# Scores of an attention kernel in half-array matmuls, and weighted values in one bank

## The chip, the cores and the metric

The kernel runs on one core of one Trainium2 chip. The metric is the device time of one execution in microseconds (us), as the median of several runs. One execution is also recorded by the hardware profiler; the profile below belongs to that one.

## The reference, cut to what matters

```python
# q, k, v: (8 batches, 12 heads, 448 positions, 64 wide), all float32
q_n, k_n = rmsnorm(q, g_q), rmsnorm(k, g_k)          # over the 64
scores = 1/8 * q_n @ k_n.T                            # 448 x 448 per head
attn = softmax(scores)
x = (attn @ v), heads side by side                    # (8*448, 768)
h = x @ w_in                                          # 768 -> 2048
g = h * clip(h + 3, 0, 6) / 6
out = g @ w_out                                       # 2048 -> 768, float32
```

There are 96 heads and, behind them, a feed-forward network on 3584 rows.

## The kernel before, in words

**Pairs.** Heads are worked on in 48 pairs: head A and head B of a pair, 6 pairs to a batch (`HP`). The 448 positions of a head are three tiles of 128 and a rest of 64 (`NT`, `REST`). k, q and v come in for two pairs at a time (`load_k`, `load_q`, `load_v`, L254 to L277, queue of SP). POOL squares, DVE sums, ACT makes the inverse root, and the normalised k and q are written as bf16.

**Transposes.** Scores need k and q with the 64 features on the partitions. For pairs 0 to 13 (`TD = 14`) PE transposes (L349) into one bank `t_ps`, and DVE or ACT copies out. From pair 14 on, that is heads 28 and later, one transposing DMA per pair does it (`transposes_dma`, L378): it takes 11 blocks of 128 x 128, seven of k and four of q, from a staging tile and puts them into one of three `kq` tiles. ACT then multiplies the transposed q by the gains (`scale_q`, L375).

**Scores.** The seven k blocks are padded: blocks 0 to 2 hold head A on partitions 0 to 63 and zeros below, blocks 4 to 6 hold head B on partitions 64 to 127 and zeros above, block 3 holds the rests of both. q has both heads, A above B. So each of seven matmuls per pair (`score`, L393, 128 keys x 448 queries, contraction over 128 partitions) gives the scores of one head, or of the two rests. POOL writes the padded blocks in two multiplications (`normalize_k`, L359), q in one (`normalize_q`, L367); the zeros are set once (`clear_kq`, L525). Scores go to two PSUM banks `sc` in turn, and ACT takes the exponential of each out of its bank (`expo`, L399, into a ring of 14 tiles `eT`).

**Weighted values.** `weigh` (L413, L419) multiplies the exponentials by v with a column of ones, for all four query tiles of a pair: 28 matmuls, in two halves of 14, into two banks `av`. `divide` (L428, L429) takes the reciprocal of the sums and multiplies, on DVE. The result `xn` is transposed into `xT` by PE for pairs 0 to 13 (`x_out`, L446, with a DVE copy, L457), by DMA from then on (`x_out_dma`, L450).

**Feed-forward.** When six pairs of a batch are done, its 16 blocks of h can run (`h_mm`, L461, six matmuls of 448 columns each), each with a clip on ACT (`relu`, L467) and a product on DVE (`gate`, L472), and then y (`y_mm`, L480, 16 matmuls of 384 columns each), copied out (L280) and stored (L491). These use three banks `m`, and at the end also the two `sc` banks. PSUM's eight banks are so: `sc` 2, `m` 3, `av` 2, `t_ps` 1.

**What sets the order.** Each engine works through a fixed list of instructions. The lists come from a planner (`Plan`, L46 to L154) that runs when the kernel is built: every step has an engine (or a choice of them), an assumed duration, the steps that it needs, and a key for its priority. `Plan.run` plays the steps through in assumed time and hands each engine what is ready. On PE, attention's steps come first and feed-forward matmuls fill the gaps, kept to a ratio (`share`); after 110 us of assumed time a PE step is taken only 500 ns after the step of another engine that it needs (`STEADY`, `SLACK`).

Of the kernel before, what the change touches and what calls it, by code (L numbers as in the profile page):

```python
# [8 lines left out]
FP32 = mybir.dt.float32  # L9
# [148 lines left out]
def kernel(  # L158
# [32 lines left out]
    TD = 14  # L191
    W4 = 4 * P
# [18 lines left out]
    kpad = [x[:, 0:7 * P] for x in kq_r]  # L211
    sq_r = ring(2, [P, GP, 8, D], FP32, "sq")
# [4 lines left out]
    qT_r = [x[:, 7 * P:7 * P + S] for x in kq_r]  # L217
    eT_r = ring(NE, [P, W4], BF16, "eT")
# [6 lines left out]
    KQ = 11 * P // 2  # L225
# [5 lines left out]
    sc_r = ring(2, [P, 512], FP32, "sc", psum)  # L231
    m_r = ring(3, [P, 512], FP32, "m", psum)
    av_ps = psum.tile([P, 4, 256], FP32, name="av")
    t_ps = psum.tile([P, 2, 4 * P], BF16, name="t_ps")
# [13 lines left out]
    def part_of(p, n):  # L248
        return (p // GP) % NS, slice(p % GP, p % GP + n)
# [12 lines left out]

    def load_k(eng, p, n):
        g, pr = part_of(p, n)
        src, st = heads(k, p, n), k_st[g][:, pr]
        eng.dma_start(
            out=st.rearrange("p r h t d -> p (r h) (t d)")[:, :, 0:NT * D], in_=blocks(src))
        for rows, x, t, rest in zip((lo, hi), (0, 0), (NT, 4), halves_of(src)):
            eng.dma_start(out=st[rows, :, x, t, :], in_=rest)
# [34 lines left out]
    def raw(a, p, n):  # L304

        g, pr = part_of(p, n)
        return (k_st, q_st)[a][g][:, pr].rearrange("p r h t d -> p r (h t) d")[:, :, 0:8, :]
# [47 lines left out]
    def normalize_k(eng, p):  # L355
        blocks = kq_st[p % NQ][:, 0:7 * P]
        for h in range(2):
            c0 = h * (NT * P)
            eng.tensor_tensor(  # L359
                out=blocks[:, c0:c0 + W4].rearrange("p (t c) -> p t c", t=4)[:, :, h * D:(h + 1) * D],  # L360
                in0=raw(0, p, 1)[:, 0, 4 * h:4 * h + 4, :],
                in1=rstd_r[(p // GP) % 2][:, 0, p % GP, 4 * h:4 * h + 4].unsqueeze(2)
                .to_broadcast([P, 4, D]), op=A_MULT,
            )

    def normalize_q(eng, p):
        eng.tensor_tensor(  # L367
            out=kq_st[p % NQ][:, 7 * P:11 * P].rearrange("p (t h d) -> p h t d", t=4, h=2),
            in0=raw(1, p, 1).rearrange("p r (h t) d -> p (r h) t d", h=2),
            in1=rstd_r[(p // GP) % 2][:, 1, p % GP, :].rearrange("p (h t) -> p h t", h=2)  # L370
            .unsqueeze(3).to_broadcast([P, 2, 4, D]), op=A_MULT,
        )

    def scale_q(p):
        nc.scalar.activation(out=qT_r[p % NK], in_=qT_r[p % NK], func=COPY, scale=gprime[:])  # L375

    def transposes_dma(p):
        nc.sync.dma_start_transpose(  # L378
            out=kq_r[p % NK][:].rearrange("p (t c) -> p t c", c=P), in_=kq_st[p % NQ])

    def put_q(eng, p):
        if eng is nc.scalar:
            eng.activation(out=qT_r[p % NK], in_=t_ps[:, 1, 0:S], func=COPY, scale=gprime[:])
        else:
            eng.tensor_scalar_mul(qT_r[p % NK], t_ps[:, 1, 0:S], gprime[:])
# [6 lines left out]
    def score(p, i, n):  # L392
        nc.tensor.matmul(  # L393
            out=sc_r[n % 2][:, 0:S], lhsT=kpad[p % NK][:, i * P:(i + 1) * P],
            rhs=qT_r[p % NK], start=True, stop=True,
        )
# [7 lines left out]

    def weigh(p, half):
        va = vaug[p % NV]
        e = {i: eT_r[(7 * p + n) % NE] for n, i in enumerate(ORDER)}
        for i in (2 * half, 2 * half + 1):


            c0 = i * P if (p // HP) % 2 == 0 else (i * P - P if i else S - P)
            cols = slice(c0, c0 + P)
            nc.tensor.matmul(  # L413
                out=av_ps[:, i, 0:2 * W], lhsT=e[3][:, cols], rhs=va[:, 3].rearrange("p h d -> p (h d)"),
                start=True, stop=False, skip_group_check=True,
            )
            for t in range(NT):
                for h in range(2):
                    nc.tensor.matmul(  # L419
                        out=av_ps[:, i, h * W:(h + 1) * W], lhsT=e[4 * h + t][:, cols],  # L420
                        rhs=va[:, t, h], start=False, stop=(t == NT - 1 and h == 1),
                        skip_group_check=True,
                    )

    def divide(p):
        av4 = av_ps[:, :, 0:2 * W].rearrange("p n (h d) -> p n h d", h=2)
        rden = rden_r[p % 2]
        nc.vector.reciprocal(out=rden[:].unsqueeze(3), in_=av4[:, :, :, D:W])  # L428
        nc.vector.tensor_tensor(  # L429
            out=xn_r[p % NQ][:].rearrange("p n (h d) -> p n h d", h=2), in0=av4[:, :, :, 0:D],  # L430
            in1=rden[:].unsqueeze(3).to_broadcast([P, 4, 2, D]), op=A_MULT,
        )

    x_ps = t_ps[:].rearrange("p a c -> p (a c)")
# [90 lines left out]
    def clear_kq(eng, i):  # L525
        blocks = kq_st[i][:, 0:7 * P].rearrange("p (t c) -> p t c", c=P)
        eng.memset(blocks[:, 0:NT, D:P], 0.0)
        eng.memset(blocks[:, NT + 1:7, 0:D], 0.0)
# [11 lines left out]
    def at(xs, i):  # L540
        return xs[i] if 0 <= i < len(xs) else None

    sums, rst, nrm, vc, tr, pq, pk, scs, exs, wgh, div, xo, px = (
        [] for _ in range(13))

    def x_stage(p):
        b = p // HP
        if p >= TD:
            xo.append(plan.dma_transpose((p + 2, 0), 2 * P * W4, lambda: x_out_dma(p),
                               [div[p]] + h_ops.get(b - NX, [])[-1:]))  # L550
            px.append(xo[p])
            return
        xo.append(add((p + 2, 0), [("PE", 220, lambda: x_out(p))],
                      [div[p], at(px, p - 1)] + ([pq[p + 2], pk[2 * p + 4], pk[2 * p + 5]] if p >= HP else []),
# [92 lines left out]
    ckq = [by((2 * TD, 0), 600, 350, lambda e, i=i: clear_kq(e, i), w_ops[-NW:]) for i in range(NQ)]  # L647
# [4 lines left out]
    for p in range(NPAIR):  # L652
        g = p // GP
        if p % GP == 0:

            old = [nrm[i] for i in range(2 * (p - NS * GP), 2 * (p - NS * GP) + 2 * GP)] if g >= NS else [clr[g]]
            oldv = vc[p - NS * GP:p - NS * GP + GP] if g >= NS else [clv[g]]
# [19 lines left out]
            for j, (p0, n) in enumerate(single):  # L677
                j = min(j, len(todo) - 1)
                for a in range(2):
# [4 lines left out]
                             [(lk, lq)[a][j]] + ([squares[m - 2]] if m >= 2 else []))  # L684
# [22 lines left out]
        else:  # L707
            nrm.append(add((p - 2, 4), [("POOL", 1250, lambda p=p: normalize_k(G, p))],
                           [rstd_op[0, p], at(tr, p - NQ), ckq[p % NQ]]))
            nrm.append(add((p - 2, 4), [("POOL", 1100, lambda p=p: normalize_q(G, p))],  # L710
                           [rstd_op[1, p], at(tr, p - NQ), *w_ops[-NW:]]))
# [5 lines left out]
                      [lv[p], at(wgh, 2 * (p - NV) + 1), at(clo, p)]))  # L717

        if p >= TD:
            old = at(scs, 7 * (p - NK) + 6)  # L720
            tr.append(plan.dma_transpose((p - 1, 3), 22 * P * P, lambda p=p: transposes_dma(p),
                                         [nrm[2 * p], nrm[2 * p + 1], old]))
            pq.append(add((p - 1, 0), [("ACT", 640, lambda p=p: scale_q(p))], [tr[p], mg]))
            pk += [tr[p], tr[p]]
        else:
            tr.append(add((p - 1, 3), [("PE", 440, lambda p=p: transposes(p))],
                          [nrm[2 * p], nrm[2 * p + 1], at(px, p - 3) if p - 3 >= HP else None, at(pq, p - 1), at(pk, 2 * p - 1),
                           at(pk, 2 * p - 2)], 165))
            pq.append(add((p - 1, 0), [("DVE", 450, lambda p=p: put_q(V, p)), ("ACT", 640, lambda p=p: put_q(A_, p))],
                          [tr[p], mg, at(scs, 7 * (p - NK) + 6)]))  # L730
            for part in range(2):
                pk.append(add((p - 1, 1 + part), [("DVE", 415, lambda p=p, part=part: put_k(p, part))],
                              [tr[p], at(scs, 7 * (p - NK) + 6), at(clk, p)]))
        for n in range(7):
            i, m = ORDER[n], 7 * p + n
            scs.append(add((p, 2), [("PE", 189, lambda p=p, i=i, m=m: score(p, i, m))],
                           [pq[p], pk[2 * p], pk[2 * p + 1] if i >= 3 else None, at(exs, m - 2)], 165))
            exs.append(add((p, 1), [("ACT", 550, lambda m=m: expo(m))],
                           [scs[m], at(wgh, 2 * ((m - NE) // 7) + 1) if m >= NE else None]))
        for half in range(2):  # L740
            wgh.append(add((p + 1, 1), [("PE", 510, lambda p=p, half=half: weigh(p, half))],
                           exs[7 * p:7 * p + 7] + [vc[p], at(div, p - 1), pad], 165))
        div.append(add((p + 1, 0), [("DVE", 880, lambda p=p: divide(p))],
                       [wgh[2 * p], wgh[2 * p + 1], at(xo, p - NQ)]))
        if p >= 2:
            x_stage(p - 2)
            if p - 2 == HP - 1:
                plan.banks.append([m_r[2], px[HP - 1]])
            if p - 2 in (HP * b + HP - 1 for b in range(B - 1)):
                feed_forward((p - 2) // HP)  # L750
    x_stage(NPAIR - 2)
    x_stage(NPAIR - 1)
    plan.banks += [[m, exs[-1]] for m in sc_r]
# [35 lines left out]
```

## Time and profile before

| | us |
|---|---|
| runs shown: lowest, median, highest | 449.77, 450.78, 450.88 |
| the profiled execution's own time | 451.33 |
| its span in the profile | 449.5 |
| PE busy | 424.5 |
| ACT busy | 274.8 |
| DVE busy | 240.1 |
| POOL busy | 229.7 |
| matmuls of scores (L393): first and last start | 12.4, 364.2 |

The granted clock of TensorE was 0.995 on average. The span is what lies between the first and the last recorded instruction; the execution's own time is 1.8 us longer. Where the prediction shows lines of the profile: PE is TensorE with its matmuls, PEld its weight loads, DVE the vector engine, ACT the scalar engine, POOL GpSimd, SP the engine that issues most DMAs. A line with `xN` holds N instructions. A busy PE means that some matmul was under way; as matmuls overlap, the durations of single ones add up to more than the busy time. In the table of windows, each engine's busy time in a stretch stands with its number of instructions, then the granted clock, the share of time in which the 16 DMA engines moved data, and GB/s. In the list of waits, the columns are the waiting engine and its line, the releasing one, the total, how often, and the longest.

### The profile page before, as it was taken

What the parts mean: (1) busy time and instruction counts of PE and PEld (TensorE: products, weight loads), DVE (VectorE), ACT (ScalarE), POOL (GpSimd) and SP (SyncE); (2) the same over time, 40 slices, a digit from 0 to 9 for tenths busy, and PEclk for the clock granted to TensorE, in tenths of its full rate; (3) what the DMA queues carried; (4) which work ended last, traced back from release to release, by engine and by line L of the source; (5) the groups of instructions that cost most, each with busy time, mean ns of one, the idle gap of its engine ahead of it and who ended that gap; (6) DMA issues with size and microseconds to landing.
All of it is one profiled execution on the core that took longest, in us unless ns stands there. A gap on an engine that the chain in (4) does not pass through costs nothing.

```text
span 449.5 us, 9164 instructions
## 1 busy us (share of the span) xinstructions
PE 424.5 (94%) x3512; PEld 255.4 (57%) x3512; DVE 240.1 (53%) x428; ACT 274.8 (61%) x581; POOL 229.7 (51%) x251
## 2 busy tenths in 40 slices
PE   0888799899999989999999999999999999999996
PEld 0455366565566555666566565656565655555563
DVE  6899888845474346646444555453433253343321
ACT  2678678853487678878776777777767551132100
POOL 5899999958577766855667467552310000000000
PEclk9999899999999999999999999999999999999999
DMA  6899999981999999999899777955545210110021
GB/s 160 208 295 247 306 294 283 309 296 47 216 229 191 227 231 199 169 232 188 160 184 219 177 176 171 223 140 76 93 106 72 73 26 36 61 45 36 24 83 70
DMA packets 140908, 73.94 MB, mean 164 GB/s; under 512 B 90176, under 2 KB 137280, under 8 KB 140864
## 3 DMA queue, kind: packets, MB, share of 16 engines
q1 hardware_dynamic: 139232, 72.44, 69.3%
q10 hardware_dynamic: 1632, 0.92, 0.8%
q8 instruction: 27, 0.44, 0.4%
q14 instruction: 17, 0.14, 0.1%
HBM read 45.61 MB, written 11.01 MB: 126 GB/s over the span
## 4 chain that ended last, share of the span: by engine, by line
PE 84%; DMA 6%; POOL 2%; DVE 2%; ACT 2%; SPq 1%; issue 1%; POOLq 0%
PE m L461 29%; PE m L480 26%; PE sc L393 11%; PE av L419 7%; PE sc L480 5%; DMA k_st<-in_k_dram 4%; DMA kq<-w_st 3%; PE sc L461 3%; PE av L413 2%; ACT eT L399 2%; POOL qk L333 1%; POOL sq L315 1%; DVE vaug L280 1%; PE t_ps L349 1%; SPq L277 0%
## 5 line engine op out<-in xcount | busy, mean ns | idle before, releaser
L399 ACT ACTIVATE eT<-sc 128x448 bf16<-128x448 f32 x336 | 175.7, 542 | 48.6 <-PE sc L393 44.6
L461 PE MATMUL m<-xT,w_in_sb 128*128 128x448 bf16 x708 | 165.7, 355 | 0.2
L480 PE MATMUL m<-w_out_sb,gT 128*128 128x384 bf16 x768 | 150.0, 326 | 0.0
L393 PE MATMUL sc<-kq 128*128 128x448 bf16 x336 | 115.9, 359 | 8.2 <-ACT eT L399 6.4
L480 PEld LDWEIGHTS <-gT 128*128 128x128 bf16 x896 | 87.2, 98 | 62.3 <-issue 0.5
L461 PEld LDWEIGHTS <-w_in_sb 128*128 128x128 bf16 x768 | 74.1, 98 | 68.8 <-issue 6.0
L472 DVE SCALAR_TENSOR_TENSOR gT<-t_sb,m 128x448 bf16<-128x448 f32 x118 | 73.0, 620 | 72.9 <-ACT t_sb L467 72.4
L467 ACT ACTIVATE t_sb<-m 128x448 f32<-128x448 f32 x118 | 63.7, 541 | 47.3 <-PE m L461 44.3
L318 DVE TENSOR_REDUCE ssq<-sq 128x16 f32<-128x1024 f32 (+1 forms) x56 | 58.3, 1058 | 8.4 <-POOL sq L315 7.1
L359 POOL TENSOR_TENSOR w_st<-k_st,rstd 128x256 bf16<-128x256 f32 x68 | 40.2, 612 | 41.3 <-DMA kq<-w_st 40.6
L280 DVE COPY y_sb<-m 128x384 f32<-128x384 f32 x39 | 21.7, 557 | 61.4 <-PE m L480 61.2
L419 PE MATMUL av<-vaug,eT 128*128 128x65 bf16 x1152 | 54.5, 194 | 0.0
L419 PEld LDWEIGHTS <-eT 128*128 128x128 bf16 x1152 | 50.8, 99 | 4.4 <-issue 0.4
L315 POOL TENSOR_TENSOR sq<-k_st 128x1024 f32<-128x1024 f32 (+1 forms) x24 | 42.4, 1765 | 12.7 <-DMA k_st<-in_k_dram 5.9
L315 POOL TENSOR_TENSOR sq<-q_st 128x1024 f32<-128x1024 f32 (+1 forms) x26 | 44.5, 1710 | 7.1 <-DMA q_st<-in_q_dram 3.5
L393 PEld LDWEIGHTS <-kq 128*128 128x128 bf16 x336 | 31.3, 99 | 27.0 <-issue 4.9
L413 PE MATMUL av<-vaug,eT 128*128 128x130 bf16 x192 | 42.7, 222 | 0.0
L280 POOL CAST vaug<-v_st 128x512 bf16<-128x512 f32 x29 | 17.9, 618 | 45.2 <-PE av L419 44.6
L367 POOL TENSOR_TENSOR w_st<-q_st,rstd 128x512 bf16<-128x512 f32 x34 | 35.4, 1042 | 0.0
L429 DVE TENSOR_TENSOR xn<-av,rden 128x512 bf16<-128x512 f32 x48 | 33.2, 691 | 1.7
L428 DVE RECIPROCAL rden<-av 128x8 f32<-128x8 f32 x48 | 9.8, 205 | 34.1 <-PE av L419 33.7
L375 ACT ACTIVATE kq<-kq,gprime 128x448 bf16<-128x448 bf16 x34 | 22.6, 663 | 5.1 <-DMA kq<-w_st 5.1
(55 smaller groups left out, 222.5 us busy)
## 6 DMA issues: line engine op xcount, KB each, us to landing
out_dram<-y_sb SPq DMA_DIRECT2D x24, 384.0 KB, 2.9
k_st<-in_k_dram SPq DMA_DIRECT2D x23, 384.0 KB, 4.6
v_st<-in_v_dram SPq DMA_DIRECT2D x23, 384.0 KB, 4.6
q_st<-in_q_dram SPq DMA_DIRECT2D x22, 384.0 KB, 4.7
w_st<-in_moe_w_in_dram SPq DMA_DIRECT2D x8, 768.0 KB, 7.6
w_st<-in_moe_w_out_dram SPq DMA_DIRECT2D x8, 768.0 KB, 7.1
out_dram<-y_sb SPq DMA_DIRECT2D x8, 192.0 KB, 2.7
k_st<-in_k_dram SPq DMA_DIRECT2D x46, 32.0 KB, 3.9
```

What stands on the lines that cost most here:

```text
L280: (eng.copy if eng is nc.scalar else eng.tensor_copy)(out=out, in_=in_)
L315: eng.tensor_tensor(out=sq, in0=x, in1=x, op=A_MULT)
L318: nc.vector.tensor_reduce(out=ssq_r[(p // GP) % 2][:, a, p % GP:p % GP + n, :].rearrange("p r s -> p (r s)"), in_=sq_r[m][:, 0:n].rearrang ...
L359: eng.tensor_tensor(out=blocks[:, c0:c0 + W4].rearrange("p (t c) -> p t c", t=4)[:, :, h * D:(h + 1) * D], in0=raw(0, p, 1)[:, 0, 4 * h:4 ...
L393: nc.tensor.matmul(out=sc_r[n % 2][:, 0:S], lhsT=kpad[p % NK][:, i * P:(i + 1) * P], rhs=qT_r[p % NK], start=True, stop=True,)
L399: nc.scalar.activation(out=eT_r[n % NE][:, 0:S], in_=sc_r[n % 2][:, 0:S], func=EXP, bias=0.0, scale=1.0,)
L413: nc.tensor.matmul(out=av_ps[:, i, 0:2 * W], lhsT=e[3][:, cols], rhs=va[:, 3].rearrange("p h d -> p (h d)"), start=True, stop=False, skip_ ...
L419: nc.tensor.matmul(out=av_ps[:, i, h * W:(h + 1) * W], lhsT=e[4 * h + t][:, cols], rhs=va[:, t, h], start=False, stop=(t == NT - 1 and h = ...
L461: nc.tensor.matmul(out=m[:, 0:S], lhsT=w_in_sb[:, kt, f * P:(f + 1) * P], rhs=xT[:, kt, b % NX, x_slot(b)], start=(kt == 0), stop=(kt == N ...
L467: nc.scalar.activation(out=t[:], in_=m[:, 0:S], func=RELU, bias=0.5, scale=1.0 / 6.0,)
L472: nc.vector.scalar_tensor_tensor(out=gT[:, f, (b % 2) * S:(b % 2 + 1) * S], in0=t[:], scalar=1.0, in1=m[:, 0:S], op0=A_MIN, op1=A_MULT,)
L480: nc.tensor.matmul(out=m[:, 0:n], lhsT=gT[:, f, c0:c0 + P], rhs=w_out_sb[:, f, c:c + n], start=(f == 0), stop=(f == NFT - 1),)
```

## The change

From pair 14 on, the padded k blocks go. The staging tile has four blocks of k and four of q, each with head A on the first 64 features and head B on the other 64; the transposing DMA moves 8 blocks instead of 11. Two pairs are taken together as a group. A **burst** is four matmuls over 64 rows each: for each of two key tiles, head A on rows 0 to 63 and head B on rows 64 to 127, with q of the same rows, each into a bank of its own out of four. A group has three bursts; the rests of both pairs are two matmuls over 128 rows, with zeros where head A meets head B (`clear_late` sets them in the raw k tiles). ACT takes the exponential of two banks in one instruction. The four banks are the two of `sc`, that of `t_ps`, and one of `av`; so weighted values have one bank left from pair 13 (`AD`) on, and a half must be divided before the next half is written: `divide` runs per half. The outputs of pairs 12 and 13 (`XD`) are transposed by DMA too. At the end the four score banks, not two, serve feed-forward. In the planner a burst is given 620 ns, the two rests 378, a double exponential 960, a division of a half 580.

The core of the diff:

```diff
+    XD = 12
+    AD = 13
...
-    sc_r = ring(2, [P, 512], FP32, "sc", psum)
+    ps = psum.tile([P, 5, 512], FP32, name="ps")
     m_r = ring(3, [P, 512], FP32, "m", psum)
-    av_ps = psum.tile([P, 4, 256], FP32, name="av")
-    t_ps = psum.tile([P, 2, 4 * P], BF16, name="t_ps")
+    sc_r = [ps[:, i] for i in range(4)]
+    t_ps = ps[:, 2].bitcast(BF16).rearrange("p (a c) -> p a c", a=2)
...
+    def normalize_st(eng, p, a):
         eng.tensor_tensor(
-            out=kq_st[p % NQ][:, 7 * P:11 * P].rearrange("p (t h d) -> p h t d", t=4, h=2),
-            in0=raw(1, p, 1).rearrange("p r (h t) d -> p (r h) t d", h=2),
+            out=kq_st[p % NQ][:, a * W4:a * W4 + W4].rearrange("p (t h d) -> p h t d", t=4, h=2),
+            in0=raw(a, p, 1).rearrange("p r (h t) d -> p (r h) t d", h=2),
...
     def transposes_dma(p):
         nc.sync.dma_start_transpose(
-            out=kq_r[p % NK][:].rearrange("p (t c) -> p t c", c=P), in_=kq_st[p % NQ])
+            out=kq_r[p % NK][:, 0:8 * P].rearrange("p (t c) -> p t c", c=P), in_=kq_st[p % NQ])
...
+    def burst(jobs):
+
+        for i, (p, t) in enumerate(jobs):
+            for h in range(2):
+                rows = slice(h * D, h * D + D)
+                nc.tensor.matmul(
+                    out=sc_r[2 * i + h][:, 0:S], lhsT=kT_r[p % NK][rows, t * P:(t + 1) * P],
+                    rhs=qT_r[1][p % NK][rows], start=True, stop=True,
+                )
+
+    def rests(p):
+        for i in range(2):
+            nc.tensor.matmul(
+                out=sc_r[i][:, 0:S], lhsT=kT_r[(p + i) % NK][:, NT * P:W4], rhs=qT_r[1][(p + i) % NK],
+                start=True, stop=True,
+            )
+
+    def expo2(d, i):
+        nc.scalar.activation(
+            out=e2_r[d % (NE // 2)][:, :, 0:S], in_=ps[:, 2 * i:2 * i + 2, 0:S], func=EXP, bias=0.0,
+            scale=1.0,
         )
...
     def weigh(p, half):
...
+            av = ps[:, 3 + half if p < AD else 4, 256 * (i % 2):256 * (i % 2) + 2 * W]
...
-    def divide(p):
-        av4 = av_ps[:, :, 0:2 * W].rearrange("p n (h d) -> p n h d", h=2)
-        rden = rden_r[p % 2]
-        nc.vector.reciprocal(out=rden[:].unsqueeze(3), in_=av4[:, :, :, D:W])
+    def divide(p, half):
+
+        bank, t = (ps[:, 3:5], slice(0, 4)) if half == 2 else (ps[:, 4:5], slice(2 * half, 2 * half + 2))
...
+            b0 = add((a, 2), [("PE", 620, lambda a=a: burst([(a, 0), (a, 1)]))], [pq[a], *last], 165)
+            x0 = exp2((a, 1), b0, 0, at_(0)), exp2((a, 1), b0, 1, at_(0))
+            b1 = add((a, 3), [("PE", 620, lambda a=a, p=p: burst([(a, 2), (p, 0)]))], [pq[a], pq[p], *x0], 165)
+            x1 = exp2((a, 2), b1, 0, at_(0)), exp2((a, 2), b1, 1, at_(1))
+            br = add((a, 4), [("PE", 378, lambda a=a: rests(a))], [pq[a], pq[p], x1[0]], 165)
+            xr = exp2((a, 3), br, 0, at_(0, 1))
+            b2 = add((p, 2), [("PE", 620, lambda p=p: burst([(p, 1), (p, 2)]))], [x1[1], xr], 165)
+            x2 = exp2((p, 1), b2, 0, at_(1)), exp2((p, 1), b2, 1, at_(1))
...
+                w, d = [], []
+                for half in range(2):
+                    w.append(add((p + 1, 1), [("PE", 510, lambda p=p, half=half: weigh(p, half))],
+                                 [*ex_of[p], vc[p], *(d or div[p - 1]), pad], 165))
+                    d.append(add((p + 1, 0), [("DVE", 580, lambda p=p, half=half: divide(p, half))],
+                                 [w[half], at(xo, p - NQ)]))
...
-    plan.banks += [[m, exs[-1]] for m in sc_r]
+    plan.banks += [[m, d_ops[i // 2 - 2]] for i, m in enumerate(sc_r)]
```

## The prediction, made before the changed kernel had run

> **What bounds the kernel now.** I read the page first (busy time of each engine), then the windows over the stages, then the waits of PE, then the timeline of a stretch in the middle of the change. Page, first part: engine, busy us, share of the span, instructions.
>
> ```profile
> span 449.5 us, 9164 instructions
> PE 424.5 (94%) x3512; PEld 255.4 (57%) x3512; DVE 240.1 (53%) x428; ACT 274.8 (61%) x581; POOL 229.7 (51%) x251
> PE 84%; DMA 6%; POOL 2%; DVE 2%; ACT 2%; SPq 1%; issue 1%; POOLq 0%
> ```
>
> PE is busy 94% of the time and carries 84% of the chain that ended last (third line); no other engine passes 61%. The windows (busy us of PE, its weight loads, DVE, ACT, POOL; clock; DMA share) say where PE is not the bound:
>
> ```profile
> 0.00:30.00 30.00, 16.73 (x156) 10.34 (x157) 23.19 (x64) 16.77 (x41) 23.43 (x49) 1.00 0.77 205
> 30.00:60.00 30.00, 24.90 (x261) 14.59 (x259) 27.27 (x46) 22.09 (x50) 28.76 (x23) 0.94 1.04 283
> 150.00:200.00 50.00, 48.72 (x428) 29.43 (x426) 27.41 (x43) 38.56 (x83) 34.07 (x35) 1.00 1.01 208
> 200.00:250.00 50.00, 50.00 (x440) 30.71 (x439) 25.42 (x41) 37.62 (x80) 32.13 (x35) 1.00 0.97 188
> 250.00:300.00 50.00, 50.00 (x439) 30.59 (x438) 26.73 (x42) 38.24 (x81) 29.68 (x33) 1.00 0.81 188
> ```
>
> The idle of PE lies in the first 60 us, on pairs the change hardly touches. From pair 14 on (the stage of the change, about 100 to 366 us) PE is full, and after it only feed-forward is left, again on PE. All waits of PE in the whole run are these:
>
> ```profile
> PE t_ps L349 <- DVE qk L333: 9.9, 1, 9.9
> PE sc L393 <- ACT eT L399: 6.4, 18, 0.7
> PE m L446 <- DVE xn L429: 2.4, 3, 1.7
> PE sc L393 <- DVE kq L390: 1.0, 1, 1.0
> PE t_ps L349 <- POOL qk L333: 0.3, 1, 0.3
> ```
>
> So in that stage a nanosecond of PE's stream is a nanosecond of the result: feed-forward matmuls fill every gap, and what attention takes less is followed directly by them. The prices come from the timeline:
>
> ```profile
> 199.96 0.54 PE L461 MATMUL m<-xT,w_in_sb 128*128 128x448 bf16 x2
> 200.15 0.10 PEld L393 LDWEIGHTS <-kq 128*128 128x128 bf16 x1
> 200.34 0.35 PE L393 MATMUL sc<-kq 128*128 128x448 bf16 x1
> 200.53 1.11 PE L461 MATMUL m<-xT,w_in_sb 128*128 128x448 bf16 x5
> 202.26 0.10 PEld L413 LDWEIGHTS <-eT 128*128 128x128 bf16 x1
> 202.29 0.22 PE L413 MATMUL av<-vaug,eT 128*128 128x130 bf16 x1
> ```
>
> A matmul of 448 columns is shown for 0.35 us, but the next one starts 0.19 us later (200.34 to 200.53; five take 1.11 = 0.35 + 4 x 0.19). So it occupies the stream for 189 ns, and 352 (the median of the score row) less 189 = 163 ns is a tail that the next one overlaps. Weights are loaded under the matmul before (200.15, while the two of 199.96 run), and a matmul can start 30 ns behind the start of its load (202.26, 202.29).
>
> **The change part by part.**
>
> *Scores.* Before: 34 pairs x 7 = 238 matmuls of 448 columns. After: 17 groups of two pairs, each with three bursts of four 64-row matmuls (204 in all) and two 128-row ones for the remaining 64 keys (34). The number of matmuls is the same; the whole gain is that the two halves of a burst's pair, on different rows and in different banks, run side by side. If they do, 102 matmuls vanish from the stream: 102 x 189 ns = 19.3 us.
>
> *The price of the halves.* Every burst stands between 128-row matmuls, so PE passes from whole-array to half-array work and back 51 x 2 = 102 times. The trace has no 64-row matmul, so I bound a passage. Below: 0, the stream runs on (a gain is excluded, no passage shortens a matmul). Above: the whole tail of 163 ns must leave first and then a weight load of 98 ns (its row's mean), which nothing covers, 261 ns. I take 125 ns, about the middle: most of the tail counts, because half-array work can't be put into an array still in use, but part of it is the fetch that the next instruction can do beside it, and its load costs as little as the 30 ns above. 102 x 125 = 12.8 us; the ends are 0 and 26.6 us. The change itself plans a burst at 620 ns where 2 x 189 = 378 would be the stream alone, which is 121 per passage; that is an assumption of its planner, and matters here because the fillers are laid out for it.
>
> The Trainium skill, "TensorEngine Tiling (Array Packing)", section Key Properties, states that a change of the tiling mode drains TensorE. No run here shows it yet; by it the lower end goes, and with the 163 ns tail as an estimate of the drain the passages would take 16.6 us and the scores would gain 2.7 us.
>
> *Weight loads within a burst.* The second pair's load goes into rows whose matmul still runs. In the trace that is hidden (the load at 200.15 uses the same 128 rows as the matmul running), so I book nothing; without the cover it is 51 x 98 ns = 5.0 us. The Trainium skill, "TensorE: Matmul & The Clock Gate", Part 3, says that a load overlaps running matmuls only when the row groups differ; that would add these 5.0 us, but the load at 200.15 contradicts it, and the trace decides.
>
> *Weighted values by halves (pairs 13 on).* PE's matmuls are the same (28 per pair, 1.00 us from 202.04 to 203.04). New is a wait: the second half needs the bank back from the division of the first. Behind the waiting matmul PE's whole queue stands. DVE pays two reciprocals and two multiplications where one of each stood (205 and 691 ns): between the same sum and double, 0 to 35 x 0.9 = 31 us on DVE; since 8 elements already cost 205 ns I take 35 x 0.3 = 10 us. DVE has half its time free. In PE's rebuilt order at least 1.1 us of other work lies between two halves (a burst and four feed-forward matmuls at the rates above), mostly 1.2 to 2; the tail of 167 ns, the division of a half, about 0.6 us, and perhaps a gate of 620 ns (the gating operation's row) before it come to 0.8 or 1.4 us. Some waits remain: I book 0.5 us in all; bounds below.
>
> *Exponentials.* 238 of 542 ns become 119 over two banks. Each lies between 888 (221 ns for 32 elements and 542 for 448 give 0.77 ns per element) and 1084 ns: ACT loses 0 to 23 us. ACT is busy 77% in the stage, and PE waits there for it only before 200 us: nothing on the path. A burst needs its banks emptied: the tail and two exponentials, about 2.1 us behind the last one (one exponential for the two matmuls of the rest). In the rebuilt order at least 2.27 us of other work lies between (1.70 us ahead of the rest), so I book nothing; if the cover is short by 0.2 us each, it is 10 us.
>
> *Keys, queries, transposes.* POOL: two normalisations of 612 ns become one of about 1042 (the query row): 34 x 0.18 = 6 us less. The transposing DMA moves 8 blocks for 11; its issue holds SP's queue 1.97 us and would hold it 1.43, 34 x 0.54 = 18 us less on SP, with two more output transposes of 1.23 us (pairs 12 and 13) behind which k, q and v loads and stores queue. In return 8 PE transposes of about 55 ns (0.45 us) and two DVE copies go. The keys' ring of three is now freed at the group's third or fifth step; a transpose lands in 4.7 us (median), and the rebuilt order leaves about 10 us of PE's work before its first use. All this is off PE: 0.45 us gained, nothing lost. The six clears for the old padded blocks become six others of 165 ns.
>
> **Sum**, against the profiled execution (451.33 us, span 449.5, so 1.8 us around it): -19.3 + 12.8 - 0.45 + 0.5 = -6.4 us. Its 451.33 gives 444.9; the median of the runs shown is 0.55 us lower, so I forecast 444.5 us.
>
> **The rivals.**
>
> 1. *Passages nearly free* (0 to 30 ns). For it: PE's stream shows no gaps between any two kinds of matmul. Against: all of those use the whole array. 450.8 - 19.3 + (0 to 3) = 431.5 to 434.5 us; I say 433.
> 2. *Passages dear*, the other side: tail and load both open, 261 ns. It decides from 19.3 / 102 = 189 ns per passage (one matmul's stream): above that the bursts lose more than they save. For it: loads lie ahead of their matmul by 100 to 190 ns in most rows, and none can if the passage blocks them. 450.8 - 19.3 + 26.6 = 458 us.
> 3. *The change doesn't do what it says*: the halves run one after another. Then 102 passages come on top of the old stream: +12.8 us, 463.5 us. For it: nothing shows overlap here. Against: different rows, different banks, separate operands.
> 4. *The one bank of weighted values becomes the bound.* Where a gate stands before the division (1.4 us), the closest cover of 1.1 us is short by 0.3 us; two gates make it 0.9; 68 halves at 0.15 us on average is 10 us. It decides from 6.9 / 68 = 100 ns per half. Against: PE's waits of this kind from 200 us on are zero in the trace, though its scores wait for banks in the same manner. 454 us; at half the price 449.
>
> The Trainium skill, "TensorE: Matmul & The Clock Gate", Part 3, gives 3.07 times for four matmuls of 32 rows packed in one array: it speaks against rival 3, and no trace here shows it.
>
> **How the numbers follow.** Forecast with a passage of 50 to 180 ns: 0.56, time 437 to 450. Rival 1: 0.15. Rival 2: 0.13. Rival 3: 0.05. Rival 4: 0.11. A measurement of this kernel tells a change from none at about 0.3% (1.35 us, that is 449.4 and 452.1). Faster: 0.15 and 0.52 of the forecast and 0.04 of rival 4, 0.71. Same: the forecast's end and bits of rivals 2 and 4, 0.09. Slower: 0.20. For 8 in 10 the range takes in most of rivals 1, 2 and 4 and leaves out rival 3: 433 to 456 us. The forecast's own is 437 to 450.
>
> **What would show it.** Right: starts of the two halves of a burst's pair a few ns apart and the second pair 0.19 us later; the matmul behind a burst about 0.62 us after its first start; the page's PE busy time lower, attention's last score some 10 us before 364 us, PE's waits from 150 us on near zero. Wrong in the price: the spacing from the last feed-forward start to the first half, less 163 or 189, gives the passage: near 0 rival 1, near 260 rival 2. Halves 0.19 us apart: rival 3. Waits of weighted values on DVE's multiplication: rival 4. What would make the forecast wrong without any of these is a planned order that fits badly where bursts are not 620 ns: PE then waits for ACT at the bursts.

## The result, and the profile after

The changed kernel takes 599.6 us (median) where 444.5 was forecast, in a range of 433 to 456. Against the kernel before (450.7 us) the ratio is 1.3316, with a 95% interval of 1.3285 to 1.3347. The forecast had the sign wrong. Ratios, here and below, are of the means of the timed executions, and a slow execution of the run e3 below, 450.1 us, is left out of its ratio.

The page of the changed kernel (the lines that answer to the first three shown of before):

```profile
span 597.0 us, 9146 instructions
PE 456.1 (76%) x3504; PEld 247.6 (41%) x3504; DVE 251.2 (42%) x502; ACT 265.0 (44%) x459; POOL 219.5 (37%) x214
PE 55%; ACT 19%; DVE 13%; issue 5%; DMA 4%; SPq 1%; POOL 1%; ACTq 0%; DVEq 0%; POOLq 0%
```

No engine has much more work (PE's busy time, tails and slower clock included, is 7% up, ACT's is down). PE fell from 94% to 76% of the span, and a third of the chain that ended last is now on ACT and DVE (32%, before 4%). So the time went into waits. The windows show where:

```profile
0.00:30.00 30.00, 9.85 (x67) 5.31 (x68) 15.31 (x46) 10.67 (x25) 16.03 (x42) 1.00 0.78 203
30.00:60.00 30.00, 14.21 (x96) 7.69 (x96) 11.08 (x24) 9.39 (x21) 12.62 (x12) 0.56 0.58 164
60.00:100.00 40.00, 22.89 (x155) 12.56 (x154) 16.39 (x27) 14.31 (x32) 15.54 (x11) 0.59 0.40 117
150.00:200.00 50.00, 33.93 (x236) 18.07 (x236) 16.97 (x32) 17.53 (x36) 18.87 (x16) 0.73 0.30 88
250.00:300.00 50.00, 42.33 (x381) 22.74 (x380) 27.00 (x54) 32.76 (x54) 25.20 (x22) 1.00 0.70 153
```

The reader is to see that the loss begins in the first 30 us (67 matmuls where 156 were), in pairs whose scores the change leaves as they were. All engines are idle for about half of that time or more at once, so none is the bound. In the stage of the bursts (last line) PE, which was busy 50.00 of 50, is busy 42.3.

The waits name pairs of engines that had hardly waited for each other:

```profile
DVE rden L472 <- ACT eT L424: 45.1, 29, 2.8
PE ps L401 <- ACT eT L430: 40.5, 50, 2.7
ACT eT L424 <- DVE xn L473: 40.3, 30, 2.8
PE ps L454 <- ACT eT L424: 24.2, 30, 1.3
```

The first line makes no sense by the data: the reciprocal (L472) reads the bank of weighted values, the exponential (L424) reads banks of scores, and both only read. The timeline of the early stage shows the pattern (start, duration, engine and line; in brackets the idle time and its releaser):

```profile
42.25 0.54 ACT L430 ACTIVATE eT<-ps 128x448 bf16<-128x448 f32 x1 [1.01 <-PE ps L401]
42.83 0.45 DVE L393 TENSOR_SCALAR kq<-ps,gprime 128x448 bf16<-128x448 bf16 x1 [1.04 <-ACT eT L430]
43.31 0.55 ACT L430 ACTIVATE eT<-ps 128x448 bf16<-128x448 f32 x1 [0.52 <-DVE kq L393]
43.89 0.41 DVE L398 COPY kq<-ps 64x512 bf16<-64x512 bf16 x1 [0.61 <-ACT eT L430]
44.36 0.53 PE L401 MATMUL ps<-kq 128*128 128x448 bf16 x1 [1.92 <-DVE kq L398]
44.92 0.43 DVE L398 COPY kq<-ps 64x512 bf16<-64x512 bf16 x1 [0.62 <-PE ps L401]
45.39 0.54 ACT L430 ACTIVATE eT<-ps 128x448 bf16<-128x448 f32 x1 [1.53 <-DVE kq L398]
```

Exponentials read banks 0 and 1, the copies read bank 2, the score writes bank 0 or 1; each starts some 30 to 60 ns after the one before has ended. One engine at a time works on anything called `ps`: in the whole profile no instruction of one engine on `ps` overlaps one of another engine. In the kernel before, these were the tiles `sc`, `t_ps` and `av`, and such overlaps are found 1363 times; the change made them slices of one tile.

The waits stand in the program itself, not in the chip. The lists of the two built kernels (DVE, with the engines that an instruction waits for) say so before any run:

```
before  L428 Reciprocal rden<-av 128x8 [waits PE]
        L390 TensorCopy kq<-t_ps 64x512 x2
after   L472 Reciprocal rden<-ps 128x4 [waits Activation]
        L398 TensorCopy kq<-ps 64x512 [waits Activation]
```

Leaving out the gates at the end, which need ACT's result, 0 of DVE's instructions on these banks wait for ACT before the change and 74 after it, 57 of the 83 reciprocals among them.

And yet the bursts do what they were meant to do. From the changed kernel's own timeline:

```profile
207.47 2.43 PE L505 MATMUL m<-xT,w_in_sb 128*128 128x448 bf16 x12
209.83 0.55 PE L411 MATMUL ps<-kq 64*128 64x448 bf16 x4
210.32 1.96 PE L524 MATMUL m<-w_out_sb,gT 128*128 128x384 bf16 x11
```

Four matmuls take 0.55 us of which one is 0.35, so the last starts 0.20 us after the first: the halves of a couple start together. The last feed-forward matmul ahead starts at 207.47 + 2.43 - 0.355 = 209.54, its stream ends at 209.73, and the burst starts 0.10 us later; from the burst's last start (210.03) to the next matmul are 0.29 us, 0.10 more than a stream. A burst takes 0.59 us of PE's stream, where four single matmuls take 0.76.

### The profile page after: what moved, and what is told of

Same layout as the page of the kernel before. It is cut to its first block, busy times and chain, and to the rows that moved or that the text cites. A ratio compares the mean times of both kernels' runs of the same rounds, so it can differ in the third digit from the quotient of the medians.

```text
span 597.0 us, 9146 instructions
## 1 busy us (share of the span) xinstructions
PE 456.1 (76%) x3504; PEld 247.6 (41%) x3504; DVE 251.2 (42%) x502; ACT 265.0 (44%) x459; POOL 219.5 (37%) x214
## 4 chain that ended last, share of the span: by engine, by line
PE 55%; ACT 19%; DVE 13%; issue 5%; DMA 4%; SPq 1%; POOL 1%; ACTq 0%; DVEq 0%; POOLq 0%
PE m L505 13%; PE m L524 10%; ACT eT L424 9%; ACT eT L430 8%; PE ps L401 7%; PE ps L524 6%; PE ps L460 6%; DVE xn L473 5%; PE ps L411 3%; PE ps L505 3%; PE ps L454 3%; DVE kq L398 2%; DVE gT L516 2%; DVE rden L472 2%; DMA kq<-w_st 2%
## 5 line engine op out<-in xcount | busy, mean ns | idle before, releaser
L424 ACT ACTIVATE eT<-ps 128x896 bf16<-128x896 f32 x119 | 107.9, 917 | 85.8 <-DVE xn L473 40.3
L524 PE MATMUL m<-w_out_sb,gT 128*128 128x384 bf16 x672 | 123.1, 326 | 0.0
L430 ACT ACTIVATE eT<-ps 128x448 bf16<-128x448 f32 x98 | 52.2, 544 | 94.6 <-PE ps L401 35.1
L401 PE MATMUL ps<-kq 128*128 128x448 bf16 x98 | 42.8, 458 | 57.3 <-ACT eT L430 40.5
L454 PE MATMUL ps<-vaug,eT 128*128 128x130 bf16 x192 | 44.2, 230 | 38.3 <-ACT eT L424 24.2
L472 DVE RECIPROCAL rden<-ps 128x4 f32<-128x4 f32 (+1 forms) x83 | 15.4, 186 | 113.1 <-ACT eT L424 45.1
L460 PE MATMUL ps<-vaug,eT 128*128 128x65 bf16 x1152 | 62.8, 201 | 0.0
L332 POOL TENSOR_TENSOR sq<-q_st 128x1024 f32<-128x1024 f32 (+1 forms) x25 | 42.2, 1687 | 25.0 <-DVE ssq L335 20.4
L374 POOL TENSOR_TENSOR w_st<-k_st,rstd 128x512 bf16<-128x512 f32 x34 | 35.5, 1044 | 35.7 <-DMA kq<-w_st 30.1
L524 PE MATMUL ps<-w_out_sb,gT 128*128 128x384 bf16 x224 | 40.3, 326 | 9.1 <-DVE gT L516 3.9
L473 DVE TENSOR_TENSOR xn<-ps,rden 128x256 bf16<-128x256 f32 (+1 forms) x83 | 38.7, 466 | 2.9
L374 POOL TENSOR_TENSOR w_st<-q_st,rstd 128x512 bf16<-128x512 f32 x34 | 35.8, 1052 | 0.0
```

The lines of the kernel that those rows point to most:

```text
L332: eng.tensor_tensor(out=sq, in0=x, in1=x, op=A_MULT)
L374: eng.tensor_tensor(out=kq_st[p % NQ][:, a * W4:a * W4 + W4].rearrange("p (t h d) -> p h t d", t=4, h=2), in0=raw(a, p, 1).rearrange("p r ...
L401: nc.tensor.matmul(out=sc_r[n % 2][:, 0:S], lhsT=kpad[p % NK][:, i * P:(i + 1) * P], rhs=qT_r[0][p % NK], start=True, stop=True,)
L424: nc.scalar.activation(out=e2_r[d % (NE // 2)][:, :, 0:S], in_=ps[:, 2 * i:2 * i + 2, 0:S], func=EXP, bias=0.0, scale=1.0,)
L430: nc.scalar.activation(out=eT_r[n % NE][:, 0:S], in_=sc_r[n % 2][:, 0:S], func=EXP, bias=0.0, scale=1.0,)
L454: nc.tensor.matmul(out=av, lhsT=rest[:, cols], rhs=va[:, 3].rearrange("p h d -> p (h d)"), start=True, stop=False, skip_group_check=True,)
```

## The experiments

Theory: the tile layer in which the kernel is written makes an access to a PSUM tile wait for the last access by another engine to the same tile, in whatever bank, a read after a read too. First rival: the bursts, the halves of weighted values or the new order cost the time. Medians below are from timed runs; "before" was 450.3 to 451.4 us on the same chips.

**One tile in the kernel before, and separate tiles in the changed one.** e1 makes the kernel before share its five banks:

```diff
-    sc_r = ring(2, [P, 512], FP32, "sc", psum)
-    av_ps = psum.tile([P, 4, 256], FP32, name="av")
-    t_ps = psum.tile([P, 2, 4 * P], BF16, name="t_ps")
+    ps = psum.tile([P, 5, 512], FP32, name="ps")
+    sc_r = [ps[:, i] for i in range(2)]
+    t_ps = ps[:, 2].bitcast(BF16).rearrange("p (a c) -> p a c", a=2)
+    av_ps = ps[:, 3:5].rearrange("p b (n c) -> p (b n) c", n=2)
```

> The kernel before, with one edit: its two score banks, the bank of transposes and the two banks of weighted values become slices of one tile of five banks, as in the changed kernel; 128-row scores, single exponentials and the division stay. Theory (the shared tile makes every access of one engine wait for the last access of another engine, whatever the bank): the first 14 pairs get as slow as in the changed kernel, which starts its pair 14 about 107 us late (first burst at 209.8 us), and the later pairs lose some more, so 550 us or above. Rival (the bursts, the halves of weighted values or the new order cost the time): no change, 450 to 453 us.

e2 takes the changed kernel apart again:

```diff
-    ps = psum.tile([P, 5, 512], FP32, name="ps")
+    ps = ring(5, [P, 512], FP32, "ps", psum)
...
-            out=e2_r[d % (NE // 2)][:, :, 0:S], in_=ps[:, 2 * i:2 * i + 2, 0:S], func=EXP, bias=0.0,
+        for h in range(2):
+                out=e2_r[d % (NE // 2)][:, h, 0:S], in_=ps[2 * i + h][:, 0:S], func=EXP, bias=0.0,
```

> The changed kernel with the five banks as five tiles of one bank each. An instruction cannot span two tiles, so the exponential of two banks becomes two of one bank, and the division of pairs 0 to 12 is made in two halves; bursts, halves of weighted values and the order of PE are those of the changed kernel. Theory (shared tile): the 147 us go, 440 to 452 us, with some waits for the slower exponentials. Rival (bursts and halves of weighted values): it stays above 560 us.

e3 gives each stage its own tiles. The early set is released when the first burst is laid down, and the second set takes its place:

```diff
+    sc_r = ring(2, [P, 512], FP32, "sc", psum_e)
+    av_ps = psum_e.tile([P, 2, 512], FP32, name="av")
+    t_ps = psum_e.tile([P, 2, 4 * P], BF16, name="t_ps")
...
+            early.close()
+            late.extend([psum_l.tile([P, 2, 512], FP32, name="sx"), psum_l.tile([P, 2, 512], FP32, name="sy"),
+                         psum_l.tile([P, 512], FP32, name="av1")])
```

> The changed kernel with two sets of tiles in the same five banks, one after the other: for pairs 0 to 13 the tiles of the kernel before (two score tiles, transposes, two banks of weighted values), then two score tiles of two banks and one tile for weighted values; pair 13 is weighed in two banks. Double exponentials and bursts stay. Theory (shared tile): 438 to 447 us, since in the changed kernel a burst and its two passages take 0.59 us of PE's stream (207.47 to 210.32 us) for the 0.76 of four single matmuls, 51 times 0.17 = 8.5 us less than before. Rival (bursts and halves): above 560 us.

e4 is e3 with one line changed:

```diff
-                rows = slice(h * D, h * D + D)
+                rows = slice(0, P)
```

> As e3_two_sets, but the four matmuls of a burst take all 128 rows, so each gives the sum of both heads' scores (the output is another one); number, banks and order of the matmuls stay, and there is no passage between whole and half array. Theory of the gain (halves side by side for 0.10 us per passage): 51 x 0.17 = 8.5 us slower than e3_two_sets. Rival (halves bring nothing): same or faster than e3_two_sets.

Measured: e1 628.7 us (ratio 1.3926, 1.384 to 1.4012); e2 447.4 (0.9907, 0.987 to 0.9945); e3 444.9 (0.984, 0.9776 to 0.9904); e4 451.5 (1.0013, 0.9985 to 1.004). The rival is out: e1 has no burst and is slow, e2 and e3 have all of them and are fast, all three where the theory put them. PE's waits in e3 from 100 us to the end are these:

```profile
PE sx L436 <- ACT eT L442: 1.0, 2, 0.6
PE av L472 <- DVE xn L493: 0.6, 1, 0.6
PE sy L429 <- ACT eT L442: 0.3, 1, 0.3
```

The one bank of weighted values costs PE 0.6 us in all, the four banks of scores 1.3. e4 is 6.6 us slower than e3, less than the 8.5 expected. The profiled executions, 5.3 us apart, show where the rest lies: from the first burst to the last it is 224 us in e3 (118.1 to 342.4) and 231 in e4 (116.4 to 347.7), 7 us, and between 150 and 250 us PE idles 1.2 us longer in e3 (1.9 against 0.7); together 8.2. The early stage of e3 ended 1.7 us later than e4's, which hides some of it.

**What the halves gain and what a passage costs.** e5 puts both halves on the same rows:

```diff
-                rows = slice(h * D, h * D + D)
+                rows = slice(0, D)
```

> As e3_two_sets, but both matmuls of each couple in a burst take rows 0 to 63, so that head B's scores are left out (head A's stand twice); number, size, banks, order and passages stay. If the halves run side by side only because they stand on different rows, the 102 couples follow one another: 102 x 189 ns = 19.3 us slower than e3_two_sets (444.9), about 464 us. Rival (the overlap needs no different rows, or there was none): same as e3_two_sets.

Measured: 460.0 us, 15.2 more than e3 (19.3 expected; right in kind, a fifth less). A burst of e3 and one of e5 in the two timelines, with what follows it:

```profile
197.59 0.36 PE L429 MATMUL sx<-kq 64*128 64x448 bf16 x2
197.79 0.35 PE L429 MATMUL sy<-kq 64*128 64x448 bf16 x2
198.07 0.93 PE L525 MATMUL m<-xT,w_in_sb 128*128 128x448 bf16 x4
```

```profile
201.47 0.55 PE L429 MATMUL sx<-kq 64*128 64x448 bf16 x2
201.86 0.54 PE L429 MATMUL sy<-kq 64*128 64x448 bf16 x2
202.33 0.93 PE L525 MATMUL m<-xT,w_in_sb 128*128 128x448 bf16 x4
```

In e3 a couple (head A and head B of one key tile) takes 0.36 us, as long as one matmul (the starts are 3 to 6 ns apart in all 51 bursts); in e5 0.55, one after the other. To the next feed-forward matmul it is 0.48 us in e3 and 0.86 in e5. Over all 51 bursts, the median of PE's stream for a burst and its two passages is 0.580 us in e3 and 0.955 in e5, so the halves bring 51 x 0.375 = 19.1 us of stream. The time shows less of it, mostly because PE idles 1.6 us longer in e3 between 100 and 350 us (1.9 against 0.3) and the first burst came 1.2 us earlier in e5.

e5 and e4 stream the same columns one by one and differ by the passages alone: (460.0 - 451.5) / 102 = 83 ns a passage. They ran on different chips, and by the intervals of their ratios this is good to some 30 ns only. The spacings say it more closely: the median is 96 ns ahead of a burst and 93 behind it, in e3 as in e5, and 0 in e4.

**Where the 155 us of the changed kernel against e3 lie.** e6 and e7 share one set each, and e12 adds the end:

```diff
# e6, early set
+    ps = psum_e.tile([P, 5, 512], FP32, name="ps")
+    sc_r = [ps[:, i] for i in range(2)]
# e7, second set
+            ps = psum_l.tile([P, 5, 512], FP32, name="ps")
+            late.extend([ps[:, 0:2], ps[:, 2:4], ps[:, 4]])
# e12, e7 and four score banks for feed-forward at the end
-    plan.banks += [[LateBank(i), d_ops[i - 2]] for i in range(2)]
+    plan.banks += [[LateBank(i), d_ops[i // 2 - 2]] for i in range(4)]
```

> As e3_two_sets, but the first set (pairs 0 to 13: two score banks, transposes, weighted values) is one tile of five banks; the second set stays apart. Theory (shared tile): only the early stage is slowed. The first burst started at 209.8 us in the changed kernel and at 118.1 in e3_two_sets, so 445 + 92 = 537 us. Rival (in the early stage the loss comes from elsewhere): 445 us.

> As e3_two_sets, but the second set (four score banks and the bank of weighted values, from pair 14 on) is one tile of five banks; the first set stays apart. Theory (shared tile): the changed kernel's loss against e3_two_sets is 599.6 - 444.9 = 155 us, 92 of them early, so 63 us here: 508 us. Rival (the late stage's loss is only the lateness of the early one, with feed-forward left over): 445 to 455 us.

> As e7_late_one (second set as one tile), but at the end all four score banks of that tile go to feed-forward, as in the changed kernel, instead of two. In the changed kernel 123 us lie between the last burst's start and the end of the span (473.6 to 597.0), in e7_late_one 103 (381.7 to 485.0) and in e3_two_sets 100.5, with the same number of matmuls. Theory (four banks of one tile in turn make PE wait for ACT's and DVE's accesses to the others): 20 us slower than e7_late_one, about 507 us, and the two stages and this tail then sum to the changed kernel's loss. Rival (the tail was slowed by something the early stage left): 485 to 489 us.

Measured: e6 538.7 us, 93.8 more than e3 (92 expected). e7 486.7, 41.9 more: the 63 expected were too much, because I had taken all that is not early for the stage of the bursts. e12 507.1, 20.4 more than e7 (20 expected): the missing part is the end, where feed-forward takes the four banks in turn. PE's longest waits after the last burst of the changed kernel:

```profile
PE ps L524 <- DVE gT L516: 3.9, 5, 0.8
PE ps L505 <- DVE gT L516: 3.7, 7, 0.8
PE ps L524 <- ACT t_sb L511: 3.3, 5, 0.7
PE ps L505 <- ACT t_sb L511: 2.6, 4, 0.7
```

A matmul into one bank waits for a gate or a clip that reads another. In e3 PE has no wait at all in that stretch. 93.8 + 41.9 + 20.4 = 156.1 us against the 154.7 measured (599.6 - 444.9): early pairs, late pairs and end account for the whole loss. (Against e9 below, 446.0 us, the same sum is 153.9 and the loss 153.6.)

**How little sharing is enough.** e8 and e11 start from the kernel before and join two or three banks:

```diff
# e8
-    sc_r = ring(2, [P, 512], FP32, "sc", psum)
+    sc2 = psum.tile([P, 2, 512], FP32, name="sc")
+    sc_r = [sc2[:, i] for i in range(2)]
# e11
+    avt = psum.tile([P, 3, 512], FP32, name="avt")
+    av_ps = avt[:, 0:2].rearrange("p b (n c) -> p (b n) c", n=2)
+    t_ps = avt[:, 2].bitcast(BF16).rearrange("p (a c) -> p a c", a=2)
```

> The kernel before, with its two score banks as one tile of two banks and nothing else. Theory (an access waits for the last access of another engine to the same tile, in any bank): a score must wait for the exponential just before it, not the one before that; it starts about 1.0 us after the last score instead of 0.5 in every second case, so 0.5 us for some 120 of the later scores and 0.3 to 0.8 for the 98 early ones: 500 to 570 us. Rival (only three engines at a tile, or reads of two engines, make the loss): 451 us.

> The kernel before, with its bank of transposes and its two banks of weighted values as one tile of three banks; the score banks stay apart. Only PE writes and DVE reads it, and the transposes' bank is used by pairs 0 to 13 alone. Theory (the loss comes where two engines alternate on a shared tile at a short interval): each of 14 pairs has some extra waits of a division (0.9 us) or of copies out (0.4 us each), 0.5 to 2 us a pair, 7 to 28 us slower: 458 to 479 us. Rival (these waits lie under feed-forward or other waits of the first 100 us): 451 to 455 us.

Measured: e8 524.3 us (ratio 1.1618, 1.1515 to 1.1721), e11 462.3 (1.0243, 1.0187 to 1.0298), both within what the theory expected. The two score banks alone cost 73 us: a buffer of two banks in one tile is no double buffer. The wait list of e8 shows it against the 6.4 us and 18 times of the kernel before:

```profile
PE sc L394 <- ACT eT L400: 41.1, 99, 1.1
```

This line alone is not the whole 73 us. Between the two profiles the span grew by 73.5 us: 46.1 are PE's idle time (71.1 against 25.0), and 27.4 its busy time, with the same 3512 matmuls. A matmul's tail of 163 ns counts as busy wherever the next one comes too late to overlap it, and the granted clock was 0.90 to 0.97 up to 150 us; the shares of the two were not separated.

**The idea, made well.** e9 times e3 again, and e10 changes the planned duration of a burst (`("PE", 620,` to `("PE", 580,`):

> e3_two_sets once more, timed in more rounds, as the measure for the next run and for the changed kernel's own idea. Theory of the gain: 443 to 446 us, 1.2 to 1.8% less than the kernel before. Rival (the first timing was luck): within 0.3% of the kernel before.

> As e9, with a burst planned at 580 ns instead of 620, which is what the trace of e3_two_sets shows (0.49 us from a burst's first start to the next matmul, and 0.10 us ahead of it). PE's work is the same; only the fillers move. Theory (PE's stream is what counts, and its waits after 100 us were about 2 us): the same within 0.5%, 442 to 447 us. Rival (the planned order sets the time): 1% or more either way.

Measured: e9 446.0 us (0.988, 0.984 to 0.9919), e10 446.5 (0.99, 0.9862 to 0.9938). So e3 beats both kernels, by 1.6% and 1.2% (ratios) against the kernel before in its two timings, and the planned duration of a burst makes no difference that these runs can tell.

## Why the prediction was wrong, point by point

- **The step that failed** is in the first part: "The idle of PE lies in the first 60 us, on pairs the change hardly touches." It touches each access of these pairs to the banks of scores, transposes and weighted values: five banks in four tiles became one tile, and these pairs alone lost 93.8 us by it (e6), the later ones and the end 62.3 (e12). The change part by part had no term for that, though the diff shows the new tile `ps` and the prediction used the rebuilt order of instructions, whose lists carry the waits. Reading who waits for whom there, against the list of before, would have shown 74 DVE instructions that wait for ACT without any data from it.
- No rival held it either. Rival 4 had waits on the one bank of weighted values, with 10 us; that bank cost 0.6 us once it was a tile of its own (e3), so the cover of 1.1 us and more was worked out rightly.
- *Bursts:* right. The halves overlap (e3 against e5), so rival 3 is out. A passage took 93 to 96 ns (spacings in e3 and e5; 83 by the times of e4 and e5), 125 were booked; rivals 1 and 2 (0 to 30, 261) are out. The sign "about 0.62 us after its first start" was worked out wrongly: only one of the two passages lies behind a burst's first start, so the booked 125 ns mean 0.50, and 0.48 was measured. The Trainium skill, "TensorEngine Tiling (Array Packing)", section Key Properties, has the mode change drain the engine: the trace agrees that a passage costs something, but with less than the tail of 163 ns.
- *Weight loads within a burst:* right to book nothing. The Trainium skill, "TensorE: Matmul & The Clock Gate", Part 3, in its list of what overlaps, lets a load overlap only matmuls of another row group. The traces don't agree: in e5 all four halves use the same rows, and they still follow each other at 0.19 to 0.20 us (0.55 less the 0.35 of one matmul, in one couple), so the loads stay hidden.
- *Exponentials:* 917 ns against bounds of 888 and 1084. *DVE:* 251.2 us against 240.1, 11 more where 10 were booked (reciprocals and multiplications 54.1 against 43.0). *POOL:* 1044 and 1052 ns against 1042. *Transposing DMAs:* their issue holds SP 1.33 us (median in e3) against 1.43. All off PE, as said.
- **The sum** of 444.5 us is near what the change gives with its banks kept apart (e3 444.9, e9 446.0). That it is so near is in part luck. In PE's stream the halves brought 19.1 us (19.3 booked), but the passages took 102 x 0.0945 = 9.6 us where 12.8 were booked, so the bursts gained some 3 us of stream more than the sum has; the time doesn't show them. PE's waits in e3 from 100 us on, 1.9 us, are a part of the reason, and the rest is open. (The last step of the sum gives 444.9 - 0.55 = 444.35 and not 444.5, a slip without weight.) The term that was missing was 25 times the gain.

## What to carry to other kernels

When a change merges PSUM tiles, ask which engines touch the merged one, and compare the waits in the built instruction lists before and after: a wait for an engine that delivers no data is the change's real price. Give each bank of a double buffer a tile of its own; where one instruction must span two banks, make those two one tile and nothing else, and if an earlier stage needs another split, use two sets of tiles one after the other. If all engines are half idle at once and take turns, look for a lock and not for a slow engine.

## What the runs showed of the hardware that was not expected

- The granted clock fell to half where PE idled: in the changed kernel it was 0.50 from 162 to 176 us (PE busy 6.7 of 14) and 1.00 from 104 to 149 (29.4 of 45), and a score is shown for 0.53 us in the one stretch and 0.35 in the other. No long pause was needed: the fall at 153 us came behind 3.4 us with PE busy 1.5, and no pause in them was longer than 1.1 us. The 1.00 in the first row of windows above does not fit its scores, which are shown for 0.53 to 0.58 us up to 26.5 us. The 98 scores of the early pairs are shown with 458 ns on average where the same 98 have 374 in e3. So the clock may have added to what the waits cost; how much of the early 94 us is the clock and how much the waits was not separated. The Trainium skill, "TensorE: Matmul & The Clock Gate", Part 1, tells of a clock that is halved after idle windows: the halved state agrees, but PE was busy for 45% of the 3.4 us before that fall.
- A passage between whole-array and half-array matmuls costs 93 to 96 ns here, about half of a 448-column matmul. A burst of two couples gains 0.18 us of PE's stream (0.580 in e3 for 0.757 in e4). By these figures, as an estimate, a single couple between two passages would gain nothing (189 ns saved, 189 paid); no run tried it.
